# Linear attention on 64-row TensorE tiles, beside a gated MLP: pairs of 64-row matmuls with 72 columns in place of 128-row matmuls with 144

## The chip, the cores and the metric

The kernel runs on one core of a Trainium2 chip. The metric is the device time of one execution in microseconds; lower is better. The kernel before takes 220.64 us, the median of 3 runs (220.44 to 220.81). A profile is one execution recorded by the hardware profiler; the one of the kernel before has a span of 219.0 us. In it PE is TensorE's matmuls, PEld its weight loads, DVE is VectorE, ACT is ScalarE, POOL is GpSimd, and SP is the engine that issues most DMA transfers.

## The reference

All tensors are bf16. S is 2048 rows, D is 512; there are 32 heads of 16 columns. Two branches work on the same x and are mixed by a gate per row.

```python
g = sigmoid((x * gate_w).sum(-1, keepdims=True))

# branch a: linear attention with a softmax feature map
q, k, v = heads(x @ wqkv)                     # each [32, 2048, 16]
pq, pk = q @ w_phi, k @ w_phi                 # w_phi: [32, 16, 16]
phi_q = concat([softmax(pq), softmax(-pq)])   # 32 features a head
phi_k = concat([softmax(pk), softmax(-pk)])
kv = einsum('bhsf,bhsd->bhfd', phi_k, v)
z  = einsum('bhsf->bhf', phi_k)
o  = (phi_q @ kv) / (phi_q . z + 1e-6)
a  = o @ wo

# branch b: gated MLP with a mixing over rows
z  = gelu(x @ w_in)                           # w_in: [512, 1376]
z1, z2 = z[:, :688], layernorm(z[:, 688:])
b  = (z1 * (w_sp @ z2 + b_sp)) @ w_out        # w_sp: [2048, 2048]

out = g * a + (1 - g) * b
```

## The kernel before

The work runs in three stages. The first (to about 48 us) makes z1 and z2, tile by tile of 128 rows, and folds w_phi into the weights of q and k. The second (to about 100 us) makes k, v and the exponentials of pk and pq, and sums kv and z in PSUM. The third, for each tile of 128 rows, multiplies w_sp with z2 in two halves of 344 columns (`gg_half`), reads the attention out of kv (`attn_tile`), and multiplies with wo and w_out (`ba_tile`). The order on TensorE and ScalarE is the program's own; on VectorE a scheduler decides it.

First stage. The weights of z2 come in four loads of two d blocks by 344 columns, on two queues; the first tiles follow them by halves. `warm_up` issues matmuls of ones that nothing reads.

```python
def load_z2w(eng, j, h):
    eng.dma_start(out=w_z2[:, 2 * h:2 * h + 2, j * HF:(j + 1) * HF],
                  in_=w_in_v[:, 2 * h:2 * h + 2, FH + j * HF:FH + (j + 1) * HF])
nc.sync.dma_start(out=xs[:, 0, :], in_=x2[0:P, :])
load_z2w(nc.scalar, 0, 0)
load_z2w(nc.sync, 0, 1)
load_z2w(nc.scalar, 1, 0)
nc.sync.dma_start(out=xs[:, 1, :], in_=x2[P:2 * P, :])
load_z2w(nc.sync, 1, 1)
nc.scalar.dma_start(out=xs[:, 2:4, :], ...)
# [...] w_z1, then x, wqkv, w_sp by transposing loads

def x_T(i):       # a tile of x transposed on TensorE, copied to xT by VectorE
    ...
def gate_T():     # gate_w as one more column of w_z2: 4 rows transposed, 4 small copies
    ...
def wphi_fold():  # 4 matmuls whose operands have 16 rows
    ...
def fold(qk, dt): # 4 matmuls of 128 columns into one PSUM bank fps
    ...
    if dt % 2 == 0:
        nc.scalar.copy(out=dst[:, dt, :], in_=fps[:, :])
    else:
        nc.vector.tensor_copy(out=dst[:, dt, :], in_=fps[:, :])

warm_up(7); x_T(0); warm_up(5, P)
zps = [psA.tile([P, 2, CH], FP32, name="zp") for _ in range(2)]
z_half(zps[0], 0, w_z2, 0, HF, lambda: x_T(1))   # x_T(1) after two of its four matmuls
gate_T(); warm_up(2, P)
z_half(zps[1], 1, w_z2, 0, HF); warm_up(2, P)
z_half(zps[0], 0, w_z2, 1, HF + 1)
z2_tile(0, zps[0])
z_half(zps[1], 1, w_z2, 1, HF + 1, lambda: x_T(2))
z2_tile(1, zps[1])
x_T(3); z2_tile(2); z2_tile(3); b_T()
for c in range(4):                # 16 tiles of rows, four at a time
    # z2 tiles, z1 tiles; folds beside them for c = 2 (k) and c = 3 (q)
    z2_norm(ts)                   # GpSimd and VectorE
```

Third stage. One group g holds 8 heads, thus 128 rows of features (a = 0 for softmax(pq), 1 for softmax(-pq)) and 128 columns of output. `kvz` is kv with zeros outside the 16x16 blocks of the heads, with 8 columns for z and 8 for the sum of the features behind it, 144 in all. The operand that is loaded as weights is `eq`, the exponentials of pq.

```python
AW = P + 16
def kvz_evac():
    for a in range(2):
        nc.vector.tensor_tensor(out=kvz[:, a * NG:(a + 1) * NG, 0:P], in0=kvacc[a][:, :, 0:P],
                                in1=mask_bd[...], op=ALU.mult)
        nc.vector.scalar_tensor_tensor(out=kvz[:, a * NG:(a + 1) * NG, P:P + 8], ...)

def attn_tile(tt):
    at = [psM.tile([P, NG, 256], FP32, name=f"at{a}", tag="kvat", bufs=2) for a in range(2)]
    for a in range(2):
        for g in range(NG):
            nc.tensor.matmul(at[a][:, g, 0:AW], lhsT=eq[a][:, g, t0:t0 + P],
                             rhs=kvz[:, a * 4 + g, :], start=True, stop=True)
        nc.vector.tensor_copy(out=sd[:, a], in_=at[a][:, :, P:P + 16])
    # VectorE: the denominator, its reciprocal, r, then m[a] = at[a] * r[a], o = m[0] + m[1];
    # o goes through a transposing DMA to oT

def ba_mm(acc, uT, oT, c0, c1):   # 4 matmuls with wo_t, 6 with w_out_t, 512 columns each
    ...
for hh in range(1, 2 * NT):
    tt, j = divmod(hh, 2)
    gg_half(tt, j)                # 16 matmuls of 344 columns
    if j == 1:
        uTs[tt] = u_T(tt)
    if j == 1 and tt >= 2:
        ba_tile(tt - 2, uTs.pop(tt - 2), oTs.pop(tt - 2))
    for k in attn_at.get(hh, ()): # tiles 0-4 after half 1, 5-9 after half 0, 10-15 a tile ahead
        oTs[k] = attn_tile(k)
ba_tile(NT - 2, ...)
ba_tile(NT - 1, ..., nsplit=2)    # each half scaled by ScalarE and sent from its queue
```

Of the kernel before, what the change touches and what calls it, by code (L numbers as in the profile page):

```python
# [14 lines left out]
P = 128  # L15
# [3 lines left out]
DH = 16  # L19
# [10 lines left out]
AW = P + 16  # L30
# [4 lines left out]
def kernel(  # L35
# [41 lines left out]
    kvz = pers.tile([P, 8, AW], BF16, name="kvz")  # L77
    bT = pers.tile([P, NT], FP32, name="bT")
# [36 lines left out]
    def load_z2w(eng, j, h):  # L115
        eng.dma_start(
            out=w_z2[:, 2 * h:2 * h + 2, j * HF:(j + 1) * HF],
            in_=w_in_v[:, 2 * h:2 * h + 2, FH + j * HF:FH + (j + 1) * HF])

    nc.sync.dma_start(out=xs[:, 0, :], in_=x2[0:P, :])  # L120
    load_z2w(nc.scalar, 0, 0)
    load_z2w(nc.sync, 0, 1)
    load_z2w(nc.scalar, 1, 0)
    nc.sync.dma_start(out=xs[:, 1, :], in_=x2[P:2 * P, :])
    load_z2w(nc.sync, 1, 1)
# [17 lines left out]
    for q in range(NCH):  # L143
# [12 lines left out]
    nc.sync.dma_start(  # L156
        out=wo_t[:, :, :], in_=A_wo.rearrange("(g p) n -> p g n", p=P)
    )
# [25 lines left out]
    for i in range(8):  # L184
        nc.gpsimd.tensor_copy(out=kvz[:, i, P + 8:P + 16], in_=mask8[:, :])
# [6 lines left out]
    def z_half(zp, tt, wt, j, n, mid=None):  # L192
        for dt in range(NDT):
            if dt == 2 and mid is not None:
                mid()
            nc.tensor.matmul(  # L196
                zp[:, j, 0:n], lhsT=xT[:, dt, tt * P:(tt + 1) * P],
                rhs=wt[:, dt, j * HF:j * HF + n],
                start=(dt == 0), stop=(dt == NDT - 1),
            )  # L200

    def z_mm(tt, wt, w):
        zp = psA.tile([P, 2, CH], FP32, name="zp")
        for dt in range(NDT):
            for j in range(2):
                n = HF if j == 0 else w - HF
                nc.tensor.matmul(  # L207
                    zp[:, j, 0:n], lhsT=xT[:, dt, tt * P:(tt + 1) * P],
                    rhs=wt[:, dt, j * HF:j * HF + n],
                    start=(dt == 0), stop=(dt == NDT - 1),  # L210
                )
        return zp

    def z2_tile(tt, zp=None):
        if zp is None:
            zp = z_mm(tt, w_z2, FH + 1)
        z2v = z2all[:, tt, :].rearrange("p (j n) -> p j n", j=2)
        nc.scalar.activation(out=z2v, in_=zp[:, :, 0:HF], func=AF.Gelu_apprx_tanh)  # L218
        nc.vector.tensor_copy(out=glog[:, tt:tt + 1], in_=zp[:, 1, HF:HF + 1])
        for j in range(2):  # L220
            nc.vector.bn_stats(out=bn6[:, tt, j, :], in_=z2v[:, j, :])  # L221
        nc.vector.bn_aggr(out=mv[:, tt, :], in_=bn6[:, tt, :, :].rearrange("p j s -> p (j s)"))
# [21 lines left out]
    wp = psF.tile([P, CH], FP32, name="wp", tag="pq", bufs=2)  # L244

    def warm_up(n, w=CH):
        for _ in range(n):
            nc.tensor.matmul(
                wp[:, 0:w], lhsT=nc.const_aps.tensor(1.0, [P, P], BF16),
                rhs=nc.const_aps.tensor(1.0, [P, w], BF16), start=True, stop=True)  # L250
# [32 lines left out]
    def fold(qk, dt):  # L283
        dst = wq_p if qk == 0 else wk_p
        fps = psF.tile([P, CH], FP32, name="fps", tag="pq", bufs=2)
        for kc in range(NDT):
            nc.tensor.matmul(
                fps[:, kc * P:(kc + 1) * P],
                lhsT=wqkT[:, qk * 4 + kc, dt * P:(dt + 1) * P],
                rhs=wphi[:, kc, :],  # L290
                start=True, stop=True,
            )
        if dt % 2 == 0:
            nc.scalar.copy(out=dst[:, dt, :], in_=fps[:, :])
        else:
            nc.vector.tensor_copy(out=dst[:, dt, :], in_=fps[:, :])  # L296

    with tc.manual_schedule(engines={mybir.EngineType.PE, mybir.EngineType.Activation}):
# [3 lines left out]
        zps = [psA.tile([P, 2, CH], FP32, name="zp") for _ in range(2)]  # L302
        z_half(zps[0], 0, w_z2, 0, HF, lambda: x_T(1))
        gate_T()
        warm_up(2, P)
        z_half(zps[1], 1, w_z2, 0, HF)
        warm_up(2, P)
        z_half(zps[0], 0, w_z2, 1, HF + 1)
        z2_tile(0, zps[0])
        z_half(zps[1], 1, w_z2, 1, HF + 1, lambda: x_T(2))  # L310
        z2_tile(1, zps[1])
        x_T(3)
# [87 lines left out]
    def kvz_evac():  # L400
        for a in range(2):
            nc.vector.tensor_tensor(
                out=kvz[:, a * NG:(a + 1) * NG, 0:P], in0=kvacc[a][:, :, 0:P],
                in1=mask_bd[:, None, :].to_broadcast([P, NG, P]), op=ALU.mult,
            )
            nc.vector.scalar_tensor_tensor(
                out=kvz[:, a * NG:(a + 1) * NG, P:P + 8], in0=kvacc[a][:, :, P:P + 8],
                scalar=0.5e-6, in1=mask8[:, None, :].to_broadcast([P, NG, 8]),
                op0=ALU.add, op1=ALU.mult,
            )  # L410
# [14 lines left out]
    def attn_tile(tt):  # L425
        t0 = tt * P
        at = [psM.tile([P, NG, 256], FP32, name=f"at{a}", tag="kvat", bufs=2) for a in range(2)]
        sd = work.tile([P, 2, NG, 16], FP32, name="sd")
        for a in range(2):
            for g in range(NG):  # L430
                nc.tensor.matmul(
                    at[a][:, g, 0:AW], lhsT=eq[a][:, g, t0:t0 + P], rhs=kvz[:, a * 4 + g, :],
                    start=True, stop=True,
                )
            nc.vector.tensor_copy(out=sd[:, a], in_=at[a][:, :, P:P + 16])
        t12 = work.tile([P, 2, NG, 8], FP32, name="t12")
        for a in range(2):
            nc.vector.tensor_tensor(
                out=t12[:, a], in0=sd[:, a, :, 0:8], in1=sd[:, 1 - a, :, 8:16], op=ALU.mult)
        den = work.tile([P, NG, 8], FP32, name="den")  # L440
        nc.vector.tensor_tensor(out=den[:], in0=t12[:, 0], in1=t12[:, 1], op=ALU.add)
        rden = work.tile([P, NG, 8], FP32, name="rden")
        nc.vector.reciprocal(out=rden[:], in_=den[:])
        r = work.tile([P, 2, NG, 8], FP32, name="r")
        m = work.tile([P, 2, D], FP32, name="m", bufs=1)
        for a in range(2):
            nc.vector.scalar_tensor_tensor(
                out=r[:, a], in0=sd[:, 1 - a, :, 8:16], scalar=g_el[:, tt:tt + 1],
                in1=rden[:], op0=ALU.mult, op1=ALU.mult,
            )  # L450
            nc.vector.tensor_tensor(
                out=m[:, a].rearrange("p (g h d) -> p g h d", g=NG, d=DH),
                in0=at[a][:, :, 0:P].rearrange("p g (h d) -> p g h d", d=DH),
                in1=r[:, a][:, :, :, None].to_broadcast([P, NG, 8, DH]),
                op=ALU.mult,
            )
# [17 lines left out]
    def ba_tile(tt, uT, oT, nsplit=1):  # L474
        w = D // nsplit
        for h in range(nsplit):
# [3 lines left out]
            nc.scalar.activation(out=ob[:, :], in_=acc[:, 0:w], func=AF.Copy, scale=g_inv[:, tt:tt + 1])  # L480
            nc.scalar.dma_start(out=out2[tt * P:(tt + 1) * P, h * w:(h + 1) * w], in_=ob[:, :])
# [3 lines left out]
    with tc.manual_schedule(engines={mybir.EngineType.PE, mybir.EngineType.Activation}):  # L485
# [23 lines left out]
        for hh in range(1, 2 * NT):  # L509
# [4 lines left out]
            if j == 1 and tt >= 2:  # L514
                ba_tile(tt - 2, uTs.pop(tt - 2), oTs.pop(tt - 2))
            for k in attn_at.get(hh, ()):
                oTs[k] = attn_tile(k)
        ba_tile(NT - 2, uTs.pop(NT - 2), oTs.pop(NT - 2))
# [31 lines left out]
```

The softmax here doesn't subtract the row's maximum and nothing guards it: scores larger than these inputs give would overflow.

## Time and profile before

Busy time by stage, from the profile's table of stretches:

| stretch, us | what | PE busy, us | DVE busy | ACT busy |
|---|---|---|---|---|
| 0 to 10 | loads, first z2 tiles | 8.31 | 2.95 | 2.30 |
| 10 to 27 | z1, z2 | 17.00 | 12.20 | 10.44 |
| 27 to 40 | z1, z2, folds | 13.00 | 8.63 | 8.63 |
| 40 to 51 | last z tiles, first k and v | 10.21 | 6.77 | 8.24 |
| 51 to 97 | k, v, pq, kv | 45.43 | 44.07 | 32.41 |
| 97 to 103 | end of kv, first mixing | 6.00 | 3.51 | 0.75 |
| 103 to 211 | mixing, attention, output | 107.08 | 70.70 | 8.93 |
| 211 to 219 | last output | 4.67 | 0.00 | 2.32 |

Busy time of matmuls is a weak guide by itself, because a recorded matmul ends some 165 ns after the next has begun: two neighbours overlap in the record. What tells is the distance from start to start. In an unbroken row it is 146 ns for 344 columns, 216 ns for 512, 62 ns for 144 and 56 ns for 128. Where it is longer, TensorE stood still. In a line of a timeline the first number is the start, the second the time from that start to the end of the last instruction merged into it, and xN says how many were merged. A bracket at the end names idle time of the engine and what ended it.

### The profile page before, as it was taken

Reading aid. Unit: us, or ns where it says so; the run is one execution under the profiler, and the core shown is the slowest. Engines: PE = TensorE matmul, PEld = TensorE weight load, DVE = VectorE, ACT = ScalarE, POOL = GpSimd, SP = SyncE. Lnnn points to the kernel's source line nnn. Section 1 sums busy time; section 2 is a strip of 40 time slices with the busy share of each in tenths; the row PEclk is TensorE's granted clock in tenths of the full one; section 3 lists DMA queues with packets and bytes.
Section 4 is the critical chain, followed back from the end, with each engine's and each line's share of the span. In section 5 each row is a group of like instructions: output and inputs, shape, how many; then the busy total and the mean of one; then the engine's idle time right before and its main releaser. Section 6 shows DMA issues by size and latency. Waiting matters only on the chain.

```text
span 219.0 us, 3717 instructions
## 1 busy us (share of the span) xinstructions
PE 211.7 (97%) x1436; PEld 130.6 (60%) x1456; DVE 148.8 (68%) x381; ACT 74.0 (34%) x120; POOL 13.8 (6%) x51
## 2 busy tenths in 40 slices
PE   8899999989999999999999999999999999999993
PEld 3566666754455555567756665656666666666653
DVE  3376776757999999985867659547648576458610
ACT  2256666678776767650001110110011001100112
POOL 7120202020000000000000000000000000000000
PEclk9999999999999999999999999999999999999998
DMA  6999999999940000000332331331343314312331
GB/s 193 258 215 198 247 260 210 251 266 265 192 148 0 3 0 0 3 3 0 63 63 57 87 61 47 84 63 38 71 87 61 77 40 77 84 36 59 77 84 49
DMA packets 71890, 22.30 MB, mean 102 GB/s; under 512 B 65936, under 2 KB 71872, under 8 KB 71872
## 3 DMA queue, kind: packets, MB, share of 16 engines
q1 hardware_dynamic: 68016, 19.33, 43.1%
q10 hardware_dynamic: 3792, 2.73, 4.2%
q8 instruction: 11, 0.18, 0.4%
q14 instruction: 7, 0.06, 0.1%
q0 software_dynamic: 64, 0.01, 0.0%
HBM read 3.71 MB, written 2.10 MB: 27 GB/s over the span
## 4 chain that ended last, share of the span: by engine, by line
PE 89%; DVE 4%; DMA 2%; ACT 2%; issue 1%; POOL 1%; SPq 0%
PE mm L415 33%; PE zp L207 13%; PE mm L472 9%; PE mm L363 6%; PE mm L391 6%; PE mm L470 6%; PE mm L346 6%; DMA xs<-in_A_x_dram 2%; PE kvacc_707 L381 2%; PE kvacc_708 L381 2%; DVE bn_83 L221 1%; PE zp L196 1%; DVE z2all L238 1%; DVE wq_p L296 1%; ACT eq_685 L396 1%
## 5 line engine op out<-in xcount | busy, mean ns | idle before, releaser
L415 PE MATMUL mm<-z2all,wspT 128*128 128x344 bf16 x512 | 78.3, 309 | 0.0
L415 PEld LDWEIGHTS <-wspT 128*128 128x128 bf16 x512 | 49.5, 98 | 23.4
L207 PEld LDWEIGHTS <-xT 128*128 128x128 bf16 x240 | 22.9, 98 | 10.8 <-DVE xT L257 0.2
L472 PE MATMUL mm<-w_out_t,uT 128*128 128x512 bf16 (+1 forms) x102 | 23.5, 366 | 0.0
L369 DVE TENSOR_TENSOR vr<-mm,rk 128x512 bf16<-128x512 f32 x32 | 21.2, 668 | 1.0 <-PE mm L363 0.9
L352 DVE TENSOR_REDUCE zk<-ek 128x64 f32<-128x1024 bf16 x16 | 19.3, 1211 | 3.4 <-ACT ek L350 3.4
L207 PE MATMUL zp<-w_z_65,xT 128*128 128x344 bf16 x128 | 20.0, 309 | 0.0
L350 ACT ACTIVATE ek<-mm 128x512 bf16<-128x512 f32 x32 | 17.3, 598 | 3.0 <-PE mm L346 2.8
L207 PE MATMUL zp<-w_z_66,xT 128*128 128x344 bf16 x112 | 17.7, 310 | 0.0
L363 PE MATMUL mm<-wv_sb,xT 128*128 128x512 bf16 x64 | 16.4, 379 | 0.4 <-ACT eq_686 L396 0.3
L346 PE MATMUL mm<-wk_p,xT 128*128 128x512 bf16 x60 | 15.9, 379 | 0.9 <-DVE wq_p L296 0.7
L470 PE MATMUL mm<-wo_t,oT 128*128 128x512 bf16 (+1 forms) x54 | 15.7, 363 | 0.7
L472 PEld LDWEIGHTS <-uT 128*128 128x128 bf16 x102 | 10.0, 98 | 10.8
L391 PE MATMUL mm<-xT,wq_p 128*128 128x512 bf16 x62 | 16.0, 379 | 0.0
L218 ACT ACTIVATE z2all<-zp 128x688 bf16<-128x688 f32 x16 | 11.9, 743 | 11.6 <-PE zp L207 6.7
L221 DVE BATCH_NORM_STATS2 bn_83<-z2all 128x6 f32<-128x344 bf16 x32 | 14.9, 502 | 0.0
L226 ACT ACTIVATE z1all<-zp 128x688 bf16<-128x688 f32 x16 | 11.9, 743 | 6.9 <-PE zp L207 6.9
L420 DVE SCALAR_TENSOR_TENSOR ucat_92<-mm,bT,z1all 128x344 bf16<-128x344 f32 x12 | 6.9, 572 | 9.9 <-PE mm L415 9.9
L396 ACT ACTIVATE eq_685<-mm 128x512 bf16<-128x512 f32 x16 | 9.6, 597 | 10.6 <-PE mm L391 9.3
L458 DVE TENSOR_TENSOR o<-m 128x512 bf16<-128x512 f32 x16 | 10.9, 680 | 0.0
L363 PEld LDWEIGHTS <-xT 128*128 128x128 bf16 x64 | 6.2, 98 | 7.8 <-issue 0.6
L391 PEld LDWEIGHTS <-wq_p 128*128 128x128 bf16 x64 | 6.3, 98 | 7.6
(221 smaller groups left out, 207.8 us busy)
## 6 DMA issues: line engine op xcount, KB each, us to landing
w_z_65<-in_B_w_in_dram SPq DMA_DIRECT2D x2, 344.0 KB, 5.2
w_out_t<-in_B_w_out_dram SPq DMA_DIRECT2D x1, 640.0 KB, 5.3
wv_sb<-in_A_wqkv_dram SPq DMA_DIRECT2D x1, 512.0 KB, 4.6
wo_t<-in_A_wo_dram SPq DMA_DIRECT2D x1, 512.0 KB, 5.7
w_z_66<-in_B_w_in_dram ACTq DMA_DIRECT2D x2, 172.0 KB, 3.3
w_z_66<-in_B_w_in_dram SPq DMA_DIRECT2D x2, 172.0 KB, 4.3
xs<-in_A_x_dram SPq DMA_DIRECT2D x2, 128.0 KB, 3.5
xs<-in_A_x_dram ACTq DMA_DIRECT2D x1, 256.0 KB, 5.3
```

Of the source, the lines that this page charges most:

```text
L207: nc.tensor.matmul(zp[:, j, 0:n], lhsT=xT[:, dt, tt * P:(tt + 1) * P], rhs=wt[:, dt, j * HF:j * HF + n], start=(dt == 0), stop=(dt == NDT ...
L218: nc.scalar.activation(out=z2v, in_=zp[:, :, 0:HF], func=AF.Gelu_apprx_tanh)
L221: nc.vector.bn_stats(out=bn6[:, tt, j, :], in_=z2v[:, j, :])
L346: nc.tensor.matmul(k_ps[:, :], lhsT=xT[:, dt, tt * P:(tt + 1) * P], rhs=wk_p[:, dt, :], start=(dt == 0), stop=(dt == NDT - 1))
L350: nc.scalar.activation(out=ek[:, a, :], in_=k_ps[:, :], func=AF.Exp, scale=1.0 - 2.0 * a)
L352: nc.vector.tensor_reduce(out=zk[:, :], in_=ek[:].rearrange("p a (h e) -> p (a h) e", e=DH), axis=AX.X, op=ALU.add,)
L363: nc.tensor.matmul(v_ps[:, :], lhsT=xT[:, dt, tt * P:(tt + 1) * P], rhs=wv_sb[:, dt, :], start=(dt == 0), stop=(dt == NDT - 1))
L369: nc.vector.tensor_tensor(out=vr[:, a, :, 0:P].rearrange("p g (h d) -> p g h d", d=DH), in0=v_ps[:, :].rearrange("p (g h d) -> p g h d", g ...
L391: nc.tensor.matmul(pq[:, :], lhsT=wq_p[:, dt, g * P:(g + 1) * P], rhs=xT[:, dt, c0:c0 + CH], start=(dt == 0), stop=(dt == NDT - 1),)
L415: nc.tensor.matmul(gp[:, 0:HF], lhsT=wspT[:, st, tt * P:(tt + 1) * P], rhs=z2all[:, st, j * HF:(j + 1) * HF], start=(st == 0), stop=(st == ...
L470: nc.tensor.matmul(acc, lhsT=oT[:, g, :], rhs=wo_t[:, g, c0:c1], start=(g == 0), stop=False)
L472: nc.tensor.matmul(acc, lhsT=uT[:, ft, :], rhs=w_out_t[:, ft, c0:c1], start=False, stop=(ft == NFT - 1))
```

## The change

The attention matmuls are cut in two by rows. A group's kv is block-diagonal by heads, so the upper 64 rows of `eq` meet only the first 64 output columns, and the lower 64 rows only the others. Each half becomes a matmul of 64 rows and 72 columns (64 + 4 for z + 4 for the feature sum), on a tile of 64 rows of the array, alternating between rows 0-63 and 64-127; the two are meant to run at the same time. Their outputs lie in different PSUM banks. The order of the output columns changes with it, and `wo_t` is loaded in four pieces to match. `kvz_evac` writes each half of the rows by itself.

Besides, the diff has smaller parts. The weights of z2 are loaded one d block at a time by whole rows of 688 columns, and the first tiles are ordered to match. The copies of the folds change engines by the parity of dt. The ones of the warm-up write to a PSUM buffer of the z tiles. In tiles 2 to 4 the output block comes after the attention. The second half of the last tile is scaled by VectorE and sent by SP.

```diff
-AW = P + 16
+AW = 72
+halves = [slice(64 * h, 64 * h + 64) for h in range(2)]
-    def load_z2w(eng, j, h):
-        eng.dma_start(out=w_z2[:, 2 * h:2 * h + 2, j * HF:(j + 1) * HF],
-            in_=w_in_v[:, 2 * h:2 * h + 2, FH + j * HF:FH + (j + 1) * HF])
+    def load_z2w(eng, dt):
+        eng.dma_start(out=w_z2[:, dt, 0:FH], in_=w_in_v[:, dt, FH:F])
-    load_z2w(nc.scalar, 0, 0); load_z2w(nc.sync, 0, 1); load_z2w(nc.scalar, 1, 0)
+    load_z2w(nc.scalar, 0); load_z2w(nc.sync, 1); load_z2w(nc.scalar, 2)
     nc.sync.dma_start(out=xs[:, 1, :], in_=x2[P:2 * P, :])
-    load_z2w(nc.sync, 1, 1)
+    load_z2w(nc.sync, 3)
[...]
-    nc.sync.dma_start(out=wo_t[:, :, :], in_=A_wo.rearrange("(g p) n -> p g n", p=P))
+    wo_v = A_wo.rearrange("(gp k h x) n -> k h x gp n", gp=2, k=2, h=2)
+    for k in range(2):
+        for h in range(2):
+            nc.sync.dma_start(out=wo_t[halves[k], 2 * h:2 * h + 2, :], in_=wo_v[k, h])
[...]
-    wp = psF.tile([P, CH], FP32, name="wp", tag="pq", bufs=2)
+    wp = psA.tile([P, 2, CH], FP32, name="zp")
[...]
-        if dt % 2 == 0:
+        if dt % 2 == 1:
             nc.scalar.copy(out=dst[:, dt, :], in_=fps[:, :])
[...]
-        [the order of halves shown above]
+        z2_tile(0, order=[(0, 0), (1, 0), (2, 0), (0, 1), (1, 1), (2, 1), (3, 0), (3, 1)],
+            mid={(2, 0): [gate_T, lambda: x_T(1)], (2, 1): [lambda: warm_up(4, P)]})
+        z2_tile(1, mid={(1, 1): [lambda: x_T(2)], (2, 1): [lambda: x_T(3)]})
[...]
 def kvz_evac():
+            for h, rows in enumerate(halves):
+                nc.vector.tensor_tensor(
+                    out=kvz[rows, us, 0:64], in0=kvacc[a][rows, :, 64 * h:64 * h + 64], ...)
+                nc.vector.scalar_tensor_tensor(
+                    out=kvz[rows, us, 64:68], in0=kvacc[a][rows, :, P + 4 * h:P + 4 * h + 4], ...)
[...]
 def attn_tile(tt):
-        at = [psM.tile([P, NG, 256], FP32, name=f"at{a}", tag="kvat", bufs=2) for a in range(2)]
+        at = [psM.tile([P, 8, P], FP32, name=f"at{a}", tag="kvat", bufs=2) for a in range(2)]
         for a in range(2):
             for g in range(NG):
-                nc.tensor.matmul(
-                    at[a][:, g, 0:AW], lhsT=eq[a][:, g, t0:t0 + P], rhs=kvz[:, a * 4 + g, :],
-                    start=True, stop=True)
-            nc.vector.tensor_copy(out=sd[:, a], in_=at[a][:, :, P:P + 16])
+                for h, rows in enumerate(halves):
+                    nc.tensor.matmul(
+                        at[a][:, 4 * h + g, 0:AW], lhsT=eq[a][rows, g, t0:t0 + P],
+                        rhs=kvz[rows, a * NG + g, :], start=True, stop=True)
+        for a in range(2):
+            nc.vector.tensor_copy(out=sd[:, a], in_=at[a][:, :, 64:72])
[...] the VectorE steps on the same numbers of elements
 def ba_tile: the second half of the last tile
+                nc.vector.tensor_scalar(out=ob[:, :], in0=acc[:, 0:w], scalar1=g_inv[...], op0=ALU.mult)
+                nc.sync.dma_start(out=dst, in_=ob[:, :])
[...]
-            if j == 1 and tt >= 2:
+            ba = j == 1 and tt >= 2
+            if ba and tt >= 5:
                 ba_tile(tt - 2, uTs.pop(tt - 2), oTs.pop(tt - 2))
             for k in attn_at.get(hh, ()):
                 oTs[k] = attn_tile(k)
+            if ba and tt < 5:
+                ba_tile(tt - 2, uTs.pop(tt - 2), oTs.pop(tt - 2))
```

## The prediction

> **What bounds the kernel now.** I read the page first: the share of each engine and the chain of work that ended last. Then I asked for time-ordered stretches where the chain leaves the matmuls, and around the attention matmuls.
>
> ```profile
> PE 211.7 (97%) x1436; PEld 130.6 (60%) x1456; DVE 148.8 (68%) x381; ACT 74.0 (34%) x120; POOL 13.8 (6%) x51
> ...
> PE 89%; DVE 4%; DMA 2%; ACT 2%; issue 1%; POOL 1%; SPq 0%
> ```
>
> TensorE is busy 97% of the span and carries 89% of the chain. So time is won only where TensorE issues fewer or shorter matmuls, or where it stands still. The attention matmuls, from the timeline of TensorE alone:
>
> ```profile
> 121.83 0.59 PE L472 MATMUL mm<-w_out_t,uT 128*128 128x512 bf16 x2
> 122.27 0.41 PE L431 MATMUL at_1554<-kvz,eq_685 128*128 128x144 bf16 x4
> 122.52 0.41 PE L431 MATMUL at_1555<-kvz,eq_686 128*128 128x144 bf16 x4
> 122.77 0.75 PE L415 MATMUL mm<-z2all,wspT 128*128 128x344 bf16 x4
> ```
>
> Read starts, not durations (the durations overlap): 122.27 to 122.52 is four matmuls, 62 ns each for 144 columns; the eight of one tile take 0.50 us, with no gap at either end. Sixteen tiles make 8.0 us, 3.6% of the span: all that the change named in the title can touch. What a change of array tile costs is visible once already, at the fold of w_phi, whose operands have only 16 rows:
>
> ```profile
> 25.32 1.33 PE L207 MATMUL zp<-w_z_65,xT 128*128 128x344 bf16 x8
> 26.59 0.39 PE L273 MATMUL wps<-wphiE,eexp 16*128 16x128 bf16 x4
> 26.91 1.20 PE L207 MATMUL zp<-w_z_66,xT 128*128 128x344 bf16 x7
> ```
>
> The last 344-column matmul of the first group starts at 25.32 + 1.33 - 0.309 (its duration) = 26.34; normally the next follows 146 ns later, here 241: 95 ns lost. The last small one starts at 26.59 + 0.39 - 0.214 = 26.77 and the next at 26.91, 146 ns where 128 columns take 56 elsewhere: 90 ns lost. Standstill that the diff touches:
>
> ```profile
> 46.09 1.56 DVE L238 TENSOR_SCALAR z2all<-z2all,mv,rstd 128x688 bf16<-128x688 bf16 x4 [1.46 <-POOL rstd L236]
> 46.21 0.74 ACT L226 ACTIVATE z1all<-zp 128x688 bf16<-128x688 f32 x1 [0.42 <-PE zp L207]
> 46.23 1.33 PE L207 MATMUL zp<-w_z_65,xT 128*128 128x344 bf16 x8
> 47.57 0.68 DVE L296 CAST wq_p<-fps 128x512 bf16<-128x512 f32 x1
> ...
> 48.30 1.02 PE L346 MATMUL mm<-wk_p,xT 128*128 128x512 bf16 x3 [0.74 <-DVE wq_p L296]
> ```
>
> The last fold of w_q was ready at about 46.4, but its copy stands behind four normalisations on VectorE. The first k tile takes over that PSUM bank, so TensorE stands still. Its last z1 matmul starts at 47.25 and the next could start at 47.40: 0.90 us lost. Later, two attention tiles stand too close:
>
> ```profile
> 131.82 0.68 DVE L451 TENSOR_TENSOR m<-at_1636,r 128x512 f32<-128x512 f32 x1
> 132.42 0.68 DVE L451 TENSOR_TENSOR m<-at_1637,r 128x512 f32<-128x512 f32 x1
> 132.56 0.24 PEld L431 LDWEIGHTS <-eq_685 128*128 128x128 bf16 x4 [0.33 <-DVE m L451]
> ...
> 133.16 0.24 PEld L431 LDWEIGHTS <-eq_686 128*128 128x128 bf16 x4 [0.36 <-DVE m L451]
> ```
>
> Tile 5 needs the PSUM of tile 4 before VectorE has read it. Against unbroken issue the starts of the two groups are 0.14 and 0.34 us late, 0.48 in all. Last, the start:
>
> ```profile
> 4.92 0.75 PE L196 MATMUL zp<-w_z_66,xT 128*128 128x344 bf16 x2
> 6.30 0.40 PE L255 MATMUL tp<-ident,xs 128*128 128x128 bf16 x4 [0.63 <-DMA xs<-in_A_x_dram]
> ```
>
> After two matmuls TensorE waits for the second tile of x; steady work (the third z2 tile) begins at 9.91.
>
> **What the Trainium skill says.** "TensorEngine Tiling (Array Packing)", Key Properties: a change of tiling mode, not of the tile alone, drains TensorE. The 95 and 90 ns above agree; the built program gives that fold a 32x128 tile, and the new attention 64x128. "TensorE: Matmul & The Clock Gate", Part 3 (packing small matmuls): matmuls on different row tiles run at the same time and start about 4 ns apart; nothing in this trace shows it. The same page, Part 1, says that start to start never falls below about 25 ns however few the columns; the shortest here is 55 ns, so neither does the trace show that. "VectorE: DVE Perf Modes", Two Vector instructions with no wait between them: an instruction whose operands start in another 32-partition group than its forerunner's waits until that one has finished. The new evacuation of kvz alternates between rows 0 and 64; this trace has no such pair.
>
> **The change part by part.**
>
> Attention. Removed: 128 matmuls of 62 ns. Added: 256 of 72 columns, each with its own weight load, alternating between the two row tiles. A tile now costs 95 ns to enter the mode, 90 ns to leave it, and sixteen pitches p. From the 144- and 344-column pitches (62 and 146 ns) a column costs 0.42 ns and a matmul about 2 ns besides, so 72 columns one after another give p = 32 ns. If the two row tiles really overlap, a pair takes little more than 32 ns. The limit then is the weight loads: on a resumed stream the second load begins about 15 ns after the first (records of 132.560 and 132.575 in the trace), so two fit in 32 ns and p is 16 to 18. Sixteen at 17 is 0.27, with the drains 0.46 us, against 0.50: a gain of 0.04 to 0.05 a tile, 0.7 to 0.8 us in all. The halved columns bring 3.7 us, and the drains take 3.0 back.
>
> Folds. Copies of odd d blocks go to ScalarE, so the last one follows the z1 activation that ends at 46.95 and is done by about 47.5 (0.58 us a copy); TensorE is due at 47.40. The k tile waits about 0.1 instead of 0.90: -0.8 us. This could be eaten by the exponentials, which still begin only at 49.64 after a table load of 1.28. I walked the first three tiles: v of the third tile starts when the exponential of pq 1 ends, 55.64 before; with pq 0 done 0.75 earlier that ends at about 54.9. VectorE needs about 2.7 us a tile against 3.07 on TensorE and stays ahead. I keep 0.75.
>
> Order of ba and attention in tiles 2 to 4. The ba block of ten 512-column matmuls (2.16 us) now lies between attention 4 and 5, whose VectorE chain is 3.2 us; 2.16 plus the 2.34 of the mixing half covers it: -0.48 us.
>
> Start. Rows of 1376 bytes replace halves of 688; in the trace's packet records one takes 60 ns against 34 each, so the three loads ahead of the second x tile save 3 x 128 x 8 ns over 16 DMA engines, 0.2 us. The order also puts three matmuls and the gate transpose before that wait, and drops a drain and some warm-ups from after it. Left between the wait and the third z2 tile are 13 matmuls at 0.146 (1.9), 12 transposes (0.7) and 4 warm-ups (0.2): 2.8, with small waits 3.0, against 3.61 before. The start is won by 0.6 + 0.2 = 0.8 us. All later stages before 47.4 are matmul-bound and shift whole.
>
> End. The second half of the last tile is scaled on VectorE and sent by SP: about 0.1 us less.
>
> Kvz. Eight VectorE instructions for four: from 0.60 us for 512 columns and 0.10 for the small one, 4 x (0.33 + 0.09) = 1.7 plus the holds, 1.8 to 2.2 against 1.4. It began at 100.33, and attention starts at 102.45: just covered, at worst +0.1. The four loads of w_o land long before use.
>
> Sum: -0.75 (0.8) -0.48 -0.8 -0.1 = -2.1 to -2.2 beside attention, and -0.75 in attention: -2.9, or 217.8 us.
>
> **The rivals.** (1) The row tiles don't overlap in this stream of load, matmul, load, matmul: p = 32, a tile 0.70 us, +0.20 each, +3.2 in all; total 221.7. For it: every matmul here follows in order by its columns, and each pair shares one queue. (2) A floor of 25 ns: a tile 0.585, +1.4 in all; total 219.9. (3) No drain between 128- and 64-row tiles: 16 x 0.185 = 3.0 us more gained, 214.8. Against it: the 16-row fold lost time at both ends. (4) The 0.75 at the folds comes back as a wait on the exponentials: +0.75 on any of these.
>
> **Range and chances.** I give overlap about 60%, the floor 20%, no overlap 15%, and the rest to no drain. The centre is moved a little up from 217.8 for the mixture: 218.2 us, and 216.5 to 221.2 should hold it 8 times in 10. Faster by 2% means under 216.2, which needs no drain or a start won by much more: 0.09. Slower by 2% is over 225.1, which needs p above 45 ns: 0.03. Within 2%: 0.88.
>
> **What would show it.** In the profile after: starts of the attention matmuls in pairs 32 to 36 ns apart, with 241 ns from the last 344-column start to the first of them, and about 120 (72 columns and 90) from their last to the next block. Weight loads that begin only after the matmul of the same row tile has ended would make rival 1 right. The first k tile should follow the last z1 matmul with hardly a gap, the third z2 tile should begin near 9.1, and no attention tile should wait for m. I'm wrong if a tile takes over 0.6 us, or if the early exponentials set the pace.

## The result, and the profile after

The changed kernel takes 219.07 us (median of 4 runs, 218.46 to 219.64) against 220.54 for the kernel before, measured beside it: a ratio of 0.9931 with a 95% interval of 0.9902 to 0.9960. Measured once more later it took 218.60 us against 220.51, a ratio of 0.9921 (0.9908 to 0.9933). So the change wins 1.5 us by the first medians and 1.9 by the second, where the prediction had said 218.2 us and a gain of 2.4.

First the page of the changed kernel: the busy time of each engine, and the chain that ended last.

```profile
PE 211.2 (97%) x1584; PEld 125.8 (58%) x1584; DVE 149.6 (69%) x386; ACT 73.4 (34%) x119; POOL 13.2 (6%) x45
...
PE 94%; DMA 3%; SPq 1%; ACT 1%; DVE 0%; issue 0%
```

TensorE is busy as long as before, and has gone from 89% to 94% of the chain: what went is waiting, not matmul time. That hides the attention, whose records still overlap. Its cost must be read from starts. This is TensorE alone around the attention of tile 4, in order of time:

```profile
121.59 4.83 PE L403 MATMUL mm<-z2all,wspT 128*128 128x344 bf16 x32
126.35 0.30 PE L420 MATMUL at_1655<-kvz,eq_682 64*128 64x72 bf16 x8
126.49 0.30 PE L420 MATMUL at_1656<-kvz,eq_683 64*128 64x72 bf16 x8
126.72 1.04 PE L460 MATMUL mm<-wo_t,oT 128*128 128x512 bf16 x4
```

Eight matmuls of 64 rows and 72 columns now start within 0.14 us. The single records of the trace show the whole pattern. For tile 5, these are the distances from start to start in ns, from the last mixing matmul ahead of it to the third one behind:

```
242 | 3 36 3 31 4 29 3 29 4 29 3 29 4 30 3 | 127 | 155 146
```

The two matmuls of a pair start 3 ns apart, the pairs 33 ns. The first distance is 146 and 95 lost on entering the mode of 64-row tiles. The last matmul of 72 columns takes 30 ns and a little, and 94 more are lost on leaving. A further 9 are lost at the second matmul behind (155 where 146 is normal; 9 to 12 over the sixteen tiles).

Where TensorE had waited 0.90 us for the last fold, the timeline of all engines now shows the copy done on ScalarE about when it is wanted:

```profile
46.52 0.58 ACT L286 CAST wq_p<-fps 128x512 bf16<-128x512 f32 x1
...
47.16 1.02 PE L332 MATMUL mm<-wk_p,xT 128*128 128x512 bf16 x4
```

The copy ends at 47.10. The last z1 matmul starts at 46.93, so the k matmul at 47.16 comes 229 ns later, 83 ns more than in an unbroken row. And the attention of tile 5 no longer waits for VectorE to have read tile 4:

```profile
127.59 1.46 PE L462 MATMUL mm<-w_out_t,uT 128*128 128x512 bf16 x6
128.89 2.50 PE L403 MATMUL mm<-z2all,wspT 128*128 128x344 bf16 x16
131.31 0.30 PE L420 MATMUL at_1725<-kvz,eq_682 64*128 64x72 bf16 x8
131.45 0.30 PE L420 MATMUL at_1726<-kvz,eq_683 64*128 64x72 bf16 x8
```

Those lines carry no bracket. The start still has waits (the bracket names what ended each):

```profile
6.40 0.40 PE L247 MATMUL tp<-ident,xs 128*128 128x128 bf16 x4 [0.98 <-DMA xs<-in_A_x_dram]
6.63 0.60 PE L198 MATMUL zp<-w_z_66,xT 128*128 128x345 bf16 x3
...
7.07 0.39 PE L240 MATMUL zp<-const-bfloat16-1.0 128*128 128x128 bf16 x4
7.69 1.04 PE L198 MATMUL zp<-w_z_66,xT 128*128 128x344 bf16 x6 [0.22 <-DMA w_z_66<-in_B_w_in_dram]
```

The second tile of x is seen at 6.40 (6.30 before), and then TensorE waits again, for the fourth d block of the weights. The chain of waits in order of time opens with that load:

```profile
2.18 5.46 DMA w_z_66<-in_B_w_in_dram
7.69 1.04 PE zp L198 x6
```

Put together as a ledger of one profile each, in us:

| part | before | after | difference |
|---|---|---|---|
| start of the third z2 tile | 9.91 | 9.59 | -0.32 |
| from there to the first k matmul | 38.39 | 37.57 | -0.82 |
| first k to first mixing matmul | 49.01 | 49.08 | +0.07 |
| first mixing to last matmul: stall of tile 5 | 0.50 | 0.00 | -0.50 |
| first mixing to last matmul: the rest, with attention | 117.59 | 117.15 | -0.44 |
| last matmul to last packet of the output | 2.01 | 2.05 | +0.04 |
| last packet to end of the span | 1.56 | 2.05 | +0.49 |
| span | 218.97 | 217.49 | -1.48 |

The surprise is the line before the last: half a microsecond behind all data work. It shows in the end of the timelines. The kernel before:

```profile
core 0 of [0], span 219.0 us
...
216.21 0.34 ACTq L481 DMA_DIRECT2D out_dram<-ob_2607  x1
```

The changed kernel:

```profile
core 0 of [0], span 217.5 us
...
213.71 0.48 DVE L475 TENSOR_SCALAR ob_2736<-mm,g_inv 128x256 bf16<-128x256 f32 x1 [5.92 <-PE mm L462]
214.22 0.38 SPq L477 DMA_DIRECT2D out_dram<-ob_2736  x1
```

From the issue of the last transfer to the end of the span it is 2.8 us before and 3.3 after, though the transfers take the same time.

### The profile page after: what moved, and what is told of

It is laid out like the page before. It is cut to its first block, busy times and chain, and to the rows that moved or that the text cites. A ratio compares the mean times of both kernels' runs of the same rounds, so it can differ in the third digit from the quotient of the medians.

```text
span 217.5 us, 3995 instructions
## 1 busy us (share of the span) xinstructions
PE 211.2 (97%) x1584; PEld 125.8 (58%) x1584; DVE 149.6 (69%) x386; ACT 73.4 (34%) x119; POOL 13.2 (6%) x45
## 4 chain that ended last, share of the span: by engine, by line
PE 94%; DMA 3%; SPq 1%; ACT 1%; DVE 0%; issue 0%
PE mm L403 35%; PE zp L198 17%; PE mm L462 10%; PE mm L460 7%; PE mm L349 6%; PE mm L377 6%; PE mm L332 6%; DMA w_z_66<-in_B_w_in_dram 3%; PE kvacc_704 L367 2%; PE kvacc_705 L367 2%; PE fps L279 1%; ACT eq_682 L382 0%; ACT eq_683 L382 0%; DVE ob_2736 L475 0%; PE tp L247 0%; SPq L123 0%
## 5 line engine op out<-in xcount | busy, mean ns | idle before, releaser
L403 PEld LDWEIGHTS <-wspT 128*128 128x128 bf16 x512 | 48.9, 98 | 24.9
L198 PEld LDWEIGHTS <-xT 128*128 128x128 bf16 x256 | 24.3, 98 | 11.8 <-DVE xT L249 0.4
L198 PE MATMUL zp<-w_z_66,xT 128*128 128x344 bf16 (+1 forms) x128 | 20.7, 310 | 0.5 <-DVE xT L249 0.2
L198 PE MATMUL zp<-w_z_65,xT 128*128 128x344 bf16 x128 | 20.0, 310 | 0.0
L460 PE MATMUL mm<-wo_t,oT 128*128 128x512 bf16 (+1 forms) x68 | 16.6, 367 | 0.0
L408 DVE SCALAR_TENSOR_TENSOR ucat_92<-mm,bT,z1all 128x344 bf16<-128x344 f32 x12 | 6.9, 574 | 11.7 <-PE mm L403 11.7
L408 DVE SCALAR_TENSOR_TENSOR ucat_93<-mm,bT,z1all 128x344 bf16<-128x344 f32 x10 | 5.7, 573 | 7.7 <-PE mm L403 7.7
L367 PEld LDWEIGHTS <-ek 128*128 128x128 bf16 x128 | 8.7, 98 | 3.4
```

Of the source, the lines that this page charges most:

```text
L198: nc.tensor.matmul(zp[:, j, 0:n], lhsT=xT[:, dt, tt * P:(tt + 1) * P], rhs=wt[:, dt, j * HF:j * HF + n], start=(dt == 0), stop=(dt == NDT ...
L367: nc.tensor.matmul(kvacc[a][:, g, 0:P + 8], lhsT=ek[:, a, g * P:(g + 1) * P], rhs=vr[:, a, g, :], start=(tt == 0 and g % 2 == 0), stop=(tt ...
L403: nc.tensor.matmul(gp[:, 0:HF], lhsT=wspT[:, st, tt * P:(tt + 1) * P], rhs=z2all[:, st, j * HF:(j + 1) * HF], start=(st == 0), stop=(st == ...
L460: nc.tensor.matmul(acc, lhsT=oT[:, g, :], rhs=wo_t[:, g, c0:c1], start=(g == 0), stop=False)
```

## The experiments

All are edits of the changed kernel. Their ratios are to the kernel before, run beside them; single points of time are from one profile each. The changed kernel alone gave medians of 219.07 and 218.60 us on two occasions, so totals from different occasions that lie half a microsecond apart are not told apart; the stages of the profiles carry the argument.

**Attention alone undone.** 128-row matmuls of 144 columns again, with the old layout of kvz, wo_t and the PSUM tiles; the rest stays changed.

```diff
-AW = 72
+AW = P + 16
-                for h, rows in enumerate(halves):
-                    nc.tensor.matmul(at[a][:, 4 * h + g, 0:AW], lhsT=eq[a][rows, g, t0:t0 + P],
-                                     rhs=kvz[rows, a * NG + g, :], ...)
+                nc.tensor.matmul(at[a][:, g, 0:AW], lhsT=eq[a][:, g, t0:t0 + P], rhs=kvz[:, a * 4 + g, :], ...)
```

> The changed kernel with its attention alone undone: 128-row matmuls of 144 columns, kvz and w_o as before; start, folds, order and tail stay changed. Theory (pairs overlap, 16.7 ns a matmul, and 0.19 us a tile goes to two drains, so that a tile takes 0.46 us against 0.50): about 0.6 us slower than the changed kernel, near 219.7; from the first attention matmul to the last matmul of all the trace grows from 111.9 to 112.5 us. Rival (the new attention gives nothing or costs, and the rest of the diff brings the whole gain): equal or faster than the changed kernel, 219.0 or less.

Measured: 219.16 us, ratio 0.9917 (0.9889 to 0.9945), not to be told from the changed kernel. The stages tell them apart. From the last start ahead to the first start behind, less one unbroken distance, every one of the 16 attention tiles takes 0.50 us with 128 rows and 0.46 with 64. From the first mixing to the last matmul it is 117.59 us against 117.15: the paired attention is worth 0.44 us. But the last packet stands 1.55 us before the end here and 2.05 in the changed kernel. By these profiles the attention that gives the change its title brings nothing in the total, because the end takes it back.

**The same row tile four times in a row.** The loops over g and h change places.

```diff
-            for g in range(NG):
-                for h, rows in enumerate(halves):
+            for h, rows in enumerate(halves):
+                for g in range(NG):
```

> The changed kernel, but a tile's matmuls first go through the four groups on rows 0-63 and then the four on rows 64-127, twice; the same 16 matmuls and the same two drains. Theory (the overlap comes from neighbours on different row tiles): within a row tile the pitch becomes 72 columns one after another, about 32 ns, 0.52 us for the sixteen in place of 0.27, so +0.25 a tile and +4 us in all, near 223. Rival (the two row tiles overlap whatever the order, because the queue looks ahead): within 0.5 us of the changed kernel.

Measured: 219.22 us, ratio 0.9925 (0.9900 to 0.9950). TensorE at tile 3, with all sixteen matmuls merged into one line:

```profile
119.05 0.45 PE L420 MATMUL at<-kvz,eq 64*128 64x72 bf16 x16
119.43 1.04 PE L460 MATMUL mm<-wo_t,oT 128*128 128x512 bf16 x4
```

Sixteen still fit in 0.38 us from the first to the block behind. A tile is 12 ns longer than with neighbours on different row tiles (0.474 us against 0.462), 0.20 us in all. The starts still come in pairs some 33 ns apart, with 13 ns inside a pair at first and 16 at the last. The order in the program hardly matters; the theory is wrong. Matmuls of 72 columns one after another on the same rows would be some 32 ns apart by the prediction's estimate, so both row tiles must have worked at once; how the queue does it the records don't show.

**Drains doubled.** For 13 tiles the first half of the attention goes ahead of the mixing half and the second half behind it: the same matmuls, with two visits to the 64-row mode for one.

```diff
+            early_at = {k: attn_mm(k, 0) for k in attn_at.get(hh, ()) if k not in (0, 5, 10)}
             gg_half(tt, j)
[...]
-                oTs[k] = attn_tile(k)
+                oTs[k] = attn_tile(k, early_at.get(k))   # only a = 1 is left to do
```

> The changed kernel, but in 13 of the 16 tiles (all but 0, 5 and 10) the matmuls of a=0 come ahead of the mixing half and those of a=1 after it, so that the array changes its tiles four times in a tile and not twice; the same matmuls otherwise. Theory (each change costs about 94 ns, whatever is behind it): 13 x 0.19 = +2.5 us, near 221.6. Rival (the gap of 95 ns at the ends of the attention is a wait for data or for PSUM, not the change of tiles): less than +0.8 us.

Measured: 222.18 us, ratio 1.0068 (1.0049 to 1.0087). TensorE around one second visit:

```profile
122.46 2.50 PE L403 MATMUL mm<-z2all,wspT 128*128 128x344 bf16 x16
124.89 0.30 PE L418 MATMUL at<-kvz,eq 64*128 64x72 bf16 x8
125.12 2.07 PE L403 MATMUL mm<-z2all,wspT 128*128 128x344 bf16 x13
```

From 124.89 to 125.12 eight matmuls cost 0.23 us where they cost 0.14 in the middle of a visit, and as much again goes before 124.89. A tile in two visits takes 2 x 0.331 us, 0.20 more than in one, 2.6 in 13; two early visits had to wait for PSUM besides (0.22 and 0.19 us), and the 9 to 12 ns behind each added visit make up most of the 0.17 that is left. First attention to last matmul is 3.17 us longer. The drain is a price per visit, however much is done in it.

**Full rows elsewhere.** Three small operands with 4 to 16 rows also run on smaller row tiles: the gate's weights, the bias, and the fold of w_phi. Here they are padded with rows of zeros to 128.

```diff
-    brow = early.tile([NT, P], BF16, name="brow")
+    brow = early.tile([P, P], BF16, name="brow")        # likewise gaterow, wphiE, eexp
+    nc.gpsimd.memset(brow[:], 0.0)                      # likewise gaterow, wphiE
-        nc.tensor.transpose(bt[:, :], brow[:, :], ident[0:NT, 0:NT])
+        nc.tensor.matmul(bt[:, :], lhsT=brow[:, :], rhs=ident[:, 0:NT], start=True, stop=True)   # likewise gt
```

> The changed kernel, with the three small operands of the first stage (gate_w with 4 rows, b_sp with 16, w_phi and its selector with 16) laid into 128 rows of zeros, so that these matmuls use the 128-row array; the result is the same. Theory (a change of array tile costs 95 and 90 to 100 ns there too): the gaps around the b_sp transpose and the w_phi fold go, -0.38 us by the end of the first stage; the gate's lies in a wait for x and brings nothing. Rival (the gaps come from the small operands' semaphores or their short matmuls): no change in those gaps.

Measured: 218.49 us (4 runs), ratio 0.9871 (0.9810 to 0.9933); the medians alone, 218.49 and 220.61, give 0.9904. TensorE at the fold, which the prediction showed with 95 and 90 ns lost:

```profile
24.27 1.91 PE L201 MATMUL zp<-w_z,xT 128*128 128x344 bf16 x12
26.02 0.39 PE L268 MATMUL wps<-wphiE,eexp 128*128 128x128 bf16 x4
26.24 1.33 PE L201 MATMUL zp<-w_z,xT 128*128 128x344 bf16 x8
```

The operation that was marked 16*128 is now 128*128, and the next block follows after 0.22 us instead of 0.32. From the third z2 tile to the first k matmul it is 37.16 us against 37.57: 0.41 for the two visits that are gone there. The end is shorter as well (1.66 us behind the last packet for 2.05), which nobody had asked for.

**Parity of the fold copies back.**

```diff
-        if dt % 2 == 1:
+        if dt % 2 == 0:
             nc.scalar.copy(out=dst[:, dt, :], in_=fps[:, :])
```

> The changed kernel with one line undone: the copies of the folded weight go to ScalarE for the even d tiles again, as before the change. Theory (the last copy was what the first k matmul waited for): the wait ahead of the first k matmul, 0.083 us in the changed kernel, is back at 0.8 to 0.9 us, and all that comes after lies 0.7 to 0.8 us later except where the wait behind the k projection in phase B shrinks: 219.6 to 219.9 us against 219.07. Rival (the fold's gain comes back as a wait on the exponentials, as the prediction feared): the first attention matmul starts within 0.2 us of the changed kernel's 101.48 us and the time is 219.1 us.

Measured: 219.55 us, ratio 0.9952 (0.9929 to 0.9974). All engines at the last copy:

```profile
46.64 0.68 DVE L288 CAST wq_p<-fps 128x512 bf16<-128x512 f32 x1
...
47.37 1.46 PE L332 MATMUL mm<-wk_p,xT 128*128 128x512 bf16 x5 [0.74 <-DVE wq_p L288]
```

The wait is back, and the third z2 tile to the first k matmul is 38.38 us for 37.57. From there to the first attention matmul it is 54.25 us here and 54.32 in the changed kernel: of the 0.81 us, 0.07 come back in the second stage. This run started 0.6 us earlier than the changed kernel's profile, so the absolute time of the first attention matmul, which the rival named, says nothing; the distance does, and it goes against the rival.

**Output block ahead of the attention in tiles 2 to 4.**

```diff
-            if ba and tt >= 5:
+            if ba:
                 ba_tile(tt - 2, uTs.pop(tt - 2), oTs.pop(tt - 2))
[...]
-            if ba and tt < 5: ...
```

> The changed kernel with one thing undone: in row tiles 2 to 4 the output projection of the tile two back is issued ahead of the attention again. Theory (the attention of tiles 4 and 5 stand too close in the changed order's absence, so that TensorE waits for an accumulator that VectorE has not read): a stall of 0.4 to 0.5 us comes back between the attention of tiles 4 and 5, first attention to last matmul is 112.3 to 112.4 us against 111.92, and the time 219.4 to 219.6 us. Rival (the stall was due to the longer 128-row attention alone and would be gone with the paired one): first attention to last matmul within 0.1 us of 111.92 and the time 219.1 us.

Measured: 219.15 us, ratio 0.9932 (0.9916 to 0.9948). TensorE at tile 5:

```profile
131.35 0.30 PE L420 MATMUL at<-kvz,eq 64*128 64x72 bf16 x8
131.90 0.30 PE L420 MATMUL at<-kvz,eq 64*128 64x72 bf16 x8 [0.24 <-DVE m L441]
```

The second group starts 0.55 us behind the first instead of 0.14: 0.41 us of stall, and 112.33 us for 111.92 from first attention to last matmul. The stall is there with either form of attention. In the total it is lost in the spread.

**Tail back on ScalarE.**

```diff
-            if h == 0:
+            if h >= 0:
                 nc.scalar.activation(out=ob[:, :], in_=acc[:, 0:w], func=AF.Copy, scale=...)
```

> The changed kernel with the tail undone: both halves of the last tile are scaled on ScalarE and stored from its queue, as before. Theory: the last matmul starts as in the changed kernel (213.4 us), the last output packet lands within 0.1 us of the changed kernel's 215.44 us, as VectorE's 0.48 us eviction gained nothing over ScalarE's 0.47 us. For the time behind the last packet (2.05 us in the changed kernel, 1.56 us before): if it is the tail's VectorE eviction and its queue that lengthen it, it falls to about 1.56 us and the time to 218.6 us; the rival, that it hangs on how many instructions each engine has in all and not on the tail, leaves it at 1.9 to 2.05 us and the time at 219.1 us.

Measured: 218.66 us, ratio 0.9920 (0.9897 to 0.9944). Its end:

```profile
213.30 0.47 ACT L472 ACTIVATE ob<-mm,g_inv 128x256 bf16<-128x256 f32 x1 [0.61 <-PE mm L462]
213.80 0.34 ACTq L473 DMA_DIRECT2D out_dram<-ob  x1
```

Last matmul to last packet: 2.01 us against 2.05. The tail on VectorE gains nothing. Last packet to end: 1.86 us, between the two outcomes that were expected; neither was right alone, as the table further down shows.

**Half-row loads with the changed order.**

```diff
-        eng.dma_start(out=w_z2[:, dt, 0:FH], in_=w_in_v[:, dt, FH:F])
+        eng.dma_start(out=w_z2[:, 2 * h:2 * h + 2, j * HF:(j + 1) * HF],
+            in_=w_in_v[:, 2 * h:2 * h + 2, FH + j * HF:FH + (j + 1) * HF])
```

> The changed kernel with one thing undone: the loads of the second half of w_in are again four half-row pieces (688 bytes a row) instead of four loads of whole rows by d block, while the order of matmuls stays the changed one. Theory of the prediction (bigger rows let the second x tile land some 0.2 us earlier): x tile 1 is seen 0.2 to 0.3 us later than the changed kernel's 6.40 us and the third z2 tile starts 0.2 us or more later than 9.59 us. Rival, from the trace of the changed kernel (bytes and the place in the queue set the landing, not the row size): x tile 1 within 0.1 us of 6.40; the third z2 tile then moves only with the landing of the last piece of these weights, 7.64 us in the changed kernel. Either way the time is 218.9 to 219.5 us.

Measured: 219.29 us, ratio 0.9944 (0.9924 to 0.9964). The second x tile is seen at 5.64, earlier than in the changed kernel, against the prediction's theory; then the order asks for the last quarter of the weights sooner, and TensorE stands from 6.2 to 7.23. From the second x tile to the third z2 tile it is 3.89 us, more than the 3.61 of the kernel before: in this profile the new order costs time without the loads by d block.

**The changed kernel again, and its start undone whole.** The second run has half-row loads, the old order of the first two z2 tiles and the old buffer of the warm-up.

```diff
-        z2_tile(0, order=[(0, 0), (1, 0), (2, 0), (0, 1), (1, 1), (2, 1), (3, 0), (3, 1)], mid=...)
+        z_half(zps[0], 0, w_z2, 0, HF, lambda: x_T(1)); gate_T(); warm_up(2, P)
+        z_half(zps[1], 1, w_z2, 0, HF); ...             # as in the kernel before
```

> The changed kernel itself once more, beside the three that follow on the same chip, as their yardstick and to see how far the start moves from one execution to the next. The programs so far that share its start had the third z2 tile at 8.99 to 9.64 us, so it may start anywhere in there; from then on every stage should be as before to 0.05 us: first attention to last matmul 111.92 us, last packet to end 2.05 us. Time 219.0 to 219.3 us.

> The changed kernel with the start undone whole: half-row loads of the second half of w_in, the order of the matmuls of the first two z2 tiles and the buffer of the warm-up as before the change. By the prediction's step (the new start is worth 0.8 us) the third z2 tile starts near 10.2 us and the median is 0.8 us above the changed kernel's of this call. By the profiles (9.91 us before, 8.99 to 9.64, mean 9.4, in the executions with the new start) it is worth 0.3 to 0.5 us, and the median is 0.3 to 0.5 us above. If the start gains nothing, the medians agree within 0.1 us.

Measured: 218.60 us, ratio 0.9921 (0.9908 to 0.9933), for the changed kernel; 218.95, ratio 0.9935 (0.9922 to 0.9947), with the start undone. That puts the new start at some 0.3 us; the intervals overlap. TensorE in the changed kernel's second profile:

```profile
5.53 0.40 PE L247 MATMUL tp<-ident,xs 128*128 128x128 bf16 x4
...
6.98 1.04 PE L198 MATMUL zp<-w_z,xT 128*128 128x344 bf16 x6 [0.30 <-DMA w_z<-in_B_w_in_dram]
```

and with the start undone:

```profile
5.49 0.40 PE L260 MATMUL tp<-ident,xs 128*128 128x128 bf16 x4
...
9.10 1.78 PE L210 MATMUL zp<-w_z,xT 128*128 128x344 bf16 x11
```

The same program saw its second x tile at 6.40 once and at 5.53 once. In all fourteen profiles of this study the last packet of that tile lands between 4.87 and 6.46 us, in no order that follows the size of the weights' rows. What does follow the program is the stretch from that moment to the third z2 tile: 3.61 us with the old start, both times; 2.84 to 3.39, with a mean of 3.16, in the ten with the new one.

**Idle memsets.** Three memsets of one column that nothing reads, on GpSimd, are added.

```diff
+    idle = early.tile([P, 3], BF16, name="idle")
+    for i in range(3):
+        nc.gpsimd.memset(idle[:, i:i + 1], 0.0)
```

> The changed kernel with work added: three memsets of one column each on GpSimd, in an unused tile, at the start. Theory (what came behind the last packet hangs on where the number of instructions of GpSimd and VectorE stands against a block of fetched instructions: with 75 on GpSimd it pauses 0.37 us longer between its last semaphores than with 78 or 80): last packet to end falls from 2.05 to 1.66 us, the time by 0.4 us against the changed kernel's of this call, with all stages before it unchanged. Rival (the shorter end of the run with padded operands came from something else in it): 2.05 us and the same time as the changed kernel.

Measured: 218.39 us (7 runs, 218.07 to 220.54), ratio 0.9924 (0.9897 to 0.9951). In the total the gain is not established. In the profile it is:

```profile
core 0 of [0], span 216.4 us
...
213.47 0.37 SPq L480 DMA_DIRECT2D out_dram<-ob  x1
```

From the last issue to the end 2.9 us for 3.3, and from the last packet 1.67 for 2.03 in the changed kernel measured beside it. With the single records of the closing instructions, and the number of instructions that each program has for the two engines (the traces hold one fewer on GpSimd and two on VectorE), the runs line up:

| run | GpSimd, VectorE instructions | last packet to end, us | GpSimd: first to second of its four closing semaphores, us | VectorE: closing semaphore to its last drain, us |
|---|---|---|---|---|
| before | 80, 446 | 1.56 | 0.08 | 0.11 |
| attention undone | 80, 447 | 1.55 | 0.08 | 0.11 |
| changed | 75, 451 | 2.05 | 0.46 | 0.47 |
| tail back | 75, 450 | 1.86 | 0.44 | 0.11 |
| idle memsets | 78, 451 | 1.67 | 0.08 | 0.47 |
| full rows elsewhere | 78, 451 | 1.66 | 0.08 | 0.46 |
| all together (below) | 78, 450 | 1.47 | 0.08 | 0.11 |

Two things are seen. GpSimd pauses some 0.37 us more between its first two closing semaphores with 75 instructions than with 78 or 80. VectorE pauses some 0.36 us more ahead of its last drain with 451 than with 446 to 450. In the length of the end the first is worth 0.39 us (2.05 to 1.66, 1.86 to 1.47) and the second 0.19 (2.05 to 1.86, 1.66 to 1.47). Neither depends on where the tail is scaled: with attention undone VectorE scales it too, and the end is short. Both counts come with the new attention itself: its layout of kvz takes two copies on GpSimd where the old one took eight, and `kvz_evac` has eight VectorE instructions for four. That the engines there wait for their last instructions to be fetched is my guess and not shown: packets of the instruction queue lie within 2 us of the end of the span in all of these profiles, but in the changed kernel none lies inside a pause. The runs show only that the length goes with the counts.

**All together.** The padding, the tail on ScalarE, and a start in which the first three d blocks of both z2 tiles go ahead of the fourth of either.

```diff
+        z_mm(0, ..., order=first, zp=zp0, ...); x_T(1); warm_up(4, P)
+        z_mm(1, ..., order=first, zp=zp1); x_T(2)
+        z_mm(0, ..., order=last, zp=zp0); z2_end(0, zp0)
+        z_mm(1, ..., order=last, zp=zp1); z2_end(1, zp1); x_T(3)
```

> The changed kernel with three edits: operands of gate, bias and folded weight padded with zeros to 128 rows (three memsets more on GpSimd), both halves of the last tile scaled on ScalarE as before, and a start in which the first three d blocks of both z2 tiles go ahead of the fourth d block of either, with four more warm-up matmuls ahead of the second x tile's. Theory: padding -0.4 us by the 16th matmul to the first k matmul, 0.37 us less behind the last packet by GpSimd and 0.17 us less by VectorE (1.55 us in all), start -0.4 us: 1.0 to 1.4 us under the changed kernel of this call, some 217.8 to 218.1 us. Rival for the start (x tile 1 and the last d block land when they land, and the matmuls before them only wait elsewhere): 0.8 to 0.95 us under it, and the third z2 tile within the 8.99 to 9.64 us of the other runs.

Measured: 218.52 us, ratio 0.9917 (0.9904 to 0.9930): no better than the changed kernel beside it. The padding (37.16 us again from the third z2 tile to the first k matmul) and the end (1.47 us) are as expected. The start is not:

```profile
6.51 0.60 PE L202 MATMUL zp<-w_z,xT 128*128 128x345 bf16 x3
7.41 0.40 PE L253 MATMUL tp<-ident,xs 128*128 128x128 bf16 x4 [0.30 <-DMA xs<-in_A_x_dram]
...
10.25 0.60 PE L202 MATMUL zp<-w_z,xT 128*128 128x344 bf16 x3
```

The second x tile is seen at 7.41, the latest of all runs, and the third z2 tile starts at 10.25. Padding (0.41 us) and end (0.56) bring 1.0 us, and the medians differ by 0.08: the start must have cost about 0.9. Both the theory and its rival were wrong. Whether this tile of x came late by chance or because of an edit is open: the run with padding alone had it second latest, at 6.80. Padding and tail with the changed kernel's own start were not run together.

## Why the prediction was right, and where its sum was off

The direction and the range held, and the mechanism of the title was right. The gain was 1.5 us in place of 2.4 (2.9 by the sum): the sum alone missed by half, and the wide range held it. The missing part lies in three terms: attention (0.3 us), start (0.5) and end (0.6).

**Attention: overlap right, size too large.** Pairs 33 ns apart (predicted 32 to 36), 16.5 ns a matmul (16 to 18), 0.46 us a tile (0.46), 241 ns from the last mixing matmul to the first of the mode (241). Rivals 1, 2 and 3 fall with that. "TensorE: Matmul & The Clock Gate", Part 3, of the Trainium skill has 4 ns between matmuls on different row tiles; measured are 3. Its Part 1 has 25 ns as the least distance of any two; here it doesn't hold between row tiles, and the measurement decides. Mis-sized was the exit: 90 ns, from the start behind the fold of w_phi. It costs 94, and 9 to 12 at the second matmul behind, which the sum left out. With that the 16 tiles bring 0.44 us and not 0.7 to 0.8.

**Folds: right.** The wait went from 0.90 to 0.083 us, as predicted (0.1). Rival 4, that the exponentials take it back, holds for 0.07 of 0.81. The total shows less of it than the profile: 219.55 us with the wait back against 219.07 on another occasion.

**Order in tiles 2 to 4: right.** -0.48 predicted, -0.50 in the ledger, 0.41 when undone alone.

**Start: about half.** I gave 0.2 us to larger rows and 0.6 to the order. The rows don't show in the landing of the second x tile: it moves by 1.6 us between executions, and half rows didn't make it late. The order seems to need them all the same (3.89 us without them, in one profile). Of the order's 0.6, 0.45 came on average (3.61 to 3.16), and 0.25 between the two profiles in which that tile is seen at 5.53 and 5.49 (3.36 and 3.61), because the new order meets the fourth d block of the weights before it has landed; I had counted matmuls and left "small waits". The medians put the start at 0.3.

**Kvz: right.** Eight instructions take from 99.27 to 101.34 us, 2.07 in all (1.8 to 2.2), and attention follows at 101.48 with no wait beyond the drain. The hold between rows 0 and 64, for which the trace before had no pair, is seen in the first of them: on the same rows the small instruction starts at 99.60, before its forerunner's end at 99.68, while the one on the other rows starts at 99.77, just after the end at 99.75. The kernel before had 0.64 us to spare there (101.81 to 102.45), this one 0.14.

**End: wrong in sign.** I predicted -0.1 for the tail on VectorE. The tail itself is 0.04 us longer, and the closing of the program 0.49. This is the largest error of the sum, and nothing in the profile before pointed to it: its own end took 1.56 us, and no engine's busy time counts it.

## What to carry to other kernels

Row tiles pay by the visit: collect what runs on them, and pad an operand of few rows when it would force a visit of its own (0.2 us each here). Price a change of mode from starts two instructions beyond its end. When an edit moves every stage as it should and the total doesn't follow, measure from the last data packet to the end of the span before doubting the stages.

## What was unexpected of the hardware

- The two row tiles overlapped in both orders of issue: 0.474 us a tile with four matmuls of the same rows in a row, 0.462 with alternating ones.
- The closing of the program took 1.47 to 2.05 us, with steps of 0.39 and 0.19 us that go with the numbers of instructions on GpSimd and VectorE; three useless memsets took 0.36 us off it.
- The landing of a 128 KB load at the start varied from 4.87 to 6.46 us between executions, for reasons that no run here separates.
